# Seven-product matmuls in one pass over all tokens: wider first product, and output halves summed by accumulating transfers

## The chip, the core and the metric

The kernel runs on one core of a Trainium2 chip. The metric is the device time of one execution in microseconds (us). In the profile, PE is TensorE's matmuls, PEld its weight loads, DVE is VectorE, ACT is ScalarE, POOL is GpSimd and SP is SyncE, which here only issues transfers. SBUF is the on-chip memory, PSUM the eight banks into which TensorE writes[...]. "L600" is line 600 of the kernel.

## The reference

A cross attention between the tokens of each batch and a small set of states, and after it an expert block with an activation of its own. All is float32. Shapes: `x` is 8 x 8 x 512 x 64 (batch, head, token, feature of a head), `state` is 8 x 8 x 32 x 64, `w_in` is 512 x 2048, `w_out` is 2048 x 512.

```python
def _attn_ref(x, state):
    scale = 1.0 / np.sqrt(D)
    a = softmax(scale * x @ state.T)              # 512 tokens read 32 states
    xread = a @ state
    a2 = softmax(scale * state @ x.T)             # 32 states read 512 tokens
    sread = a2 @ x
    return concatenate([xread, sread], axis=2)    # 544 rows of each batch

def _moe_ref(x, w_in, w_out):                     # x: 4352 rows of 512
    h = x @ w_in
    sp = np.maximum(h, 0.0) + np.log1p(np.exp(-np.abs(h)))     # softplus
    g = h * erf(sp)
    return g @ w_out
```

(Softmax is written out in the original, with the largest score taken off and 1e-9 added to the sum.)

## The kernel before

Each head has only 32 states, so for the token rows the kernel never forms `xread`. It multiplies the states into the weights, `m = state @ w_in` (256 rows of 2048 for a batch, "mixed"), and then computes `h = a @ m`, the **first product**. The **second product** is `g @ w_out`. Batch 0 runs while the weights are fetched, with plain matmuls. For batches 1 to 7 both products use a scheme for 2 x 2 blocks with **seven products** in place of eight (Strassen in Winograd's form): some sums and differences of the blocks are formed first (S1 to S4 of the left factor, T1 to T4 of the right one), and the seven products are added up to the four quadrants c11, c12, c21, c22 of the result, over partial sums m1, u2 and u3.

A unit of the loop is one batch, one half `h` of its tokens (256) and one half `g` of the expert features (1024): four units for a batch. `hidden7` makes the seven first products of a unit, each of four matmuls of 128 columns into one bank, takes them out of PSUM with ScalarE and VectorE, and applies Softplus. `finish` applies Erf and multiplies. `project7` makes the seven second products, each of four matmuls of 256 columns; they add up over both `g` in the left and right halves of four banks (`acc`), and `store7` takes the banks out once for every two units and writes the output rows. `project7` is a generator: its `yield`s mark the places where the loop puts its steps between the first products of the next unit (`between`), so that TensorE always has something to do. `accompanied` hangs other work (attention of the next batch, mixed weights, sums) at such steps, and `behind` puts instructions after given ones on their engine. The order of the instructions of an engine in this part is set when the program is made, by a scheduler, within what the dependences allow.

```python
    def combine_m(b, g):
        (X11, X12), (X21, X22) = ([m_t[b, 2 * g + j][:, e] for e in range(2)] for j in range(2))
        sx = mix.tile([P, 3, gw], F32, name="sx", bufs=2)
        S1, S2, S4 = (sx[:, k] for k in range(3))
        tt = nc.vector.tensor_tensor
        tt(S1, X21, X22, op=ALU.add)
        tt(S2, S1, X11, op=ALU.subtract)
        tt(X21, X11, X21, op=ALU.subtract)
        tt(S4, X12, S2, op=ALU.subtract)
        X[b, g] = X11, X12, S4, X22, S1, S2, X21
    # ... cut ...
    def hidden7(b, g, h, between, copy=nc.scalar.copy):
        hs = act.tile([P, 4, S], F32, name="hs")
        s = act.tile([P, 4, S], F32, name="s")
        c11, c12, c21, c22 = (hs[:, k] for k in range(4))
        m1, u2, u3 = s[:, 3], c12, c21
        def product(n, bank, first=True):
            x, y = X[b, g][n - 1], Ys[b][n - 1]
            for i in range(GF):
                q = slice(P * i, P * i + P)
                if b < B:
                    ops = [(x[:, q], y[:, h])]
                else:
                    ops = [(x[:, i // 2, k, P * (i % 2):P * (i % 2) + P], y[:, k])
                           for k in range(2)]
                for k, (lhsT, rhs) in enumerate(ops):
                    last = nc.tensor.matmul(out=bank[:, q], lhsT=lhsT, rhs=rhs,
                                            start=(first and i == 0 and k == 0),
                                            stop=(i == GF - 1 and k == len(ops) - 1),
                                            skip_group_check=not first)
            return last
        def softplus(k):
            nc.scalar.activation(out=s[:, k], in_=hs[:, k], func=ACTF.Softplus)
        add = lambda o, x, y: nc.vector.tensor_tensor(o, x, y, op=ALU.add)
        p, q = (ps_h.tile([P, S], F32, name="h") for _ in range(2))
        product(1, p)
        copy(m1, p)
        product(6, q)
        add(u2, m1, q)
        between()
        product(2, p, False)
        copy(c11, p)
        product(7, q, False)
        add(u3, m1, q)
        softplus(0)
        between()
        p, q = (ps_h.tile([P, S], F32, name="h") for _ in range(2))
        product(5, p)
        add(c22, u3, p)
        product(4, q)
        add(c21, u3, q)
        between()
        marks[:] = product(3, p, False), add(c12, u2, p)
        for k in (3, 2, 1):
            softplus(k)
        return s, hs
    # ... cut ...
    def finish(s, hs, parts=(slice(0, GF),)):
        nc.scalar.activation(out=s, in_=s, func=ACTF.Erf)
        for k in parts:
            nc.vector.tensor_tensor(s[:, k], s[:, k], hs[:, k], op=ALU.mult)
    # ... cut ...
    wb = w_out.rearrange("p (g h i) (c e) -> p g h i c e", h=2, i=GF, c=2)
    B11, B12, B21, B22 = (wb[:, :, h, :, c, :] for h in range(2) for c in range(2))
    def project7(gT, hs, g, first, last, acc, order=range(7)):
        blocks = lambda t: [t[:, k].rearrange("p (i t) -> p i t", i=GF) for k in range(4)]
        A11, A21, A12, A22 = blocks(gT)
        S1, S2, S3, S4 = blocks(hs)
        tt = nc.vector.tensor_tensor
        products = ((A12, B21, 0, 0), (A11, B11, 2, 0), (A22, T[4], 1, 0), (S2, T[2], 0, 1),
                    (S3, T[3], 2, 1), (S1, T[1], 1, 1), (S4, B22, 3, 0))
        for n, k in enumerate(order):
            lhs, rhs, bank, c = products[k]
            for i in range(GF):
                if i % 2 == 0 and n:
                    yield
                if i == 2 and n == 1:
                    tt(S1, A21, A22, op=ALU.add)
                    tt(S2, S1, A11, op=ALU.subtract)
                    tt(S3, A11, A21, op=ALU.subtract)
                    tt(S4, A12, S2, op=ALU.subtract)
                nc.tensor.matmul(out=acc[bank][:, E2 * c:E2 * c + E2], lhsT=lhs[:, i, :],
                                 rhs=rhs[:, g, i, :], start=(first and i == 0 and c == 0),
                                 stop=(last and i == GF - 1 and (c == 1 or bank == 3)))
    def store7(acc, put):
        twice = lambda t: t.unsqueeze(1).to_broadcast([P, 2, E2])
        two = lambda t: t.rearrange("p (c e) -> p c e", c=2)
        m1, u3 = (outs.tile([P, E2], F32, name=n) for n in ("m1", "u3"))
        o1, o2 = (outs.tile([P, d_model], F32, name="ot") for _ in range(2))
        c12 = o1[:, E2:]
        add = lambda o, x, y: nc.vector.tensor_tensor(o, x, y, op=ALU.add)
        nc.scalar.copy(m1, acc[2][:, 0:E2])
        add(two(o1), twice(m1), two(acc[0]))
        put(0, o1, slice(0, E2))
        add(u3, c12, acc[2][:, E2:])
        add(two(o2), twice(u3), two(acc[1]))
        put(1, o2)
        add(c12, c12, acc[1][:, E2:])
        add(c12, c12, acc[3][:, 0:E2])
        put(0, o1, slice(E2, d_model))
    def put_x(b, h):
        rows = out[TB * b:TB * b + S].rearrange("(c p) e -> c p e", p=P)
        def go(r, ot, c=slice(0, d_model)):
            nc.sync.dma_start(out=rows[2 * h + r][:, c], in_=ot[:, c])
        return go
    # ... cut ...
    def fast(b, parts, put):
        for h in range(parts):
            box = []
            def project_(gT, k, g, h, box):
                if k == 0:
                    box.extend(tiles(4))
                yield from project7(*gT, g, k == 0, k == 1, box,
                                    (0, 1, 6, 3, 2, 5, 4) if (b, h, k) == (1, 0, 0)
                                    else range(7))
                if k == 1:
                    store7(box, put(h))
            def first(k, g, h, between, *copy):
                gT = hidden7(b, g, h, between, *copy)
                if (b, h, k) == (1, 0, 0):
                    finish(*gT, (slice(2, 4), slice(0, 2)))
                else:
                    finish(*gT)
                return gT
            for k in range(2):
                g = k ^ h ^ begins(b)
                yield lambda *how, k=k, g=g, h=h: first(k, g, h, *how), \
                    lambda gT, k=k, g=g, h=h, box=box: project_(gT, k, g, h, box)
    # ... cut ...
    def accompanied(steps, side):
        for n, _ in enumerate(steps):
            if n in side:
                side[n]()
            yield
    def behind(marks, f, *args):
        with ExitStack() as order:
            for m in marks:
                order.enter_context(tc.issue_after(m.ins))
            return f(*args)
    # ... cut ...
    def pending():
        yield from seconds
        store(acc, lambda r, ot: put_x(0, r // 2)(r % 2, ot))
    for b in range(1, B + 1):
        if b < B:
            groups = fast(b, 2, lambda h, b=b: put_x(b, h))
        else:
            groups = fast(b, 1, lambda h: put_s)
        for g, (first, second) in enumerate(groups):
            side = {}
    # ... cut ...
            steps = accompanied(pending(), side)
            copy = [nc.vector.tensor_copy] if (b, g) == (1, 1) else []
            gT_ = first(lambda: next(steps), *copy)
    # ... cut ...
            done(steps)
    # ... cut ...
            def pending(gT=gT_, second=second):
                return second(gT)
    done(pending())
```

`X[b, g]` and `Ys[b]` are the seven left and right factors of the first product. `s` and `hs` are two buffers each, `ps_h` has two banks, the four `acc` banks one buffer each. `w_in` lies whole in SBUF (64 KB in each partition), `w_out` as well.

Of the kernel before, what the change touches and what calls it, by code (L numbers as in the profile page):

```python
# [16 lines left out]
def kernel(  # L17
# [47 lines left out]

    x_t = {}
# [11 lines left out]
    def in_order(begun):  # L78

        last = {}  # L80
        for i in nc.cur_bb.bb.instructions[begun:]:
# [3 lines left out]
            if i.engine in (nc.tensor.engine, nc.vector.engine, nc.scalar.engine,  # L85
                            nc.sync.engine):
                last[i.engine] = i
# [34 lines left out]
    w_in = const.tile([P, NF // 2, NK, 2 * P], F32, name="w_in")  # L122
# [31 lines left out]
    def weights_in(j):  # L154
        return weight(w_in[:, j],
                      moe_w_in[:, 2 * P * j:2 * P * j + 2 * P].rearrange("(k p) f -> p k f", p=P),
                      (NK, 2 * P))
# [32 lines left out]
    def scored(b, xT):  # L190


        s2 = [ps_at.tile([P, S], F32, name="at") for _ in range(2)]
# [8 lines left out]
    def scores(b, xT):  # L202
        s2 = scored(b, xT)
# [141 lines left out]
    def attention(b, xT=None):  # L345
# [6 lines left out]
        sc, _ = scores(b, xT)  # L352
# [32 lines left out]
        read_tokens(b, a2T, z2, *((ps_h, "h") if 1 < b < B - 1 else ()))  # L385
# [11 lines left out]
    def mixed_pair(b, gs):  # L397

        for g in gs:
            m_t[b, g] = mix.tile([P, 2, gw], F32, name="m")  # L400
        ps = [[pool.tile([P, gw], F32, name=n) for _ in range(2)]
              for pool, n in ((ps_at, "at"), (ps_h, "h"))]
        for k, g in enumerate(gs):
            for i in range(NI):
                for e in range(2):
                    r, q = slice(D * e, D * e + D), slice(Ns * i, Ns * i + Ns)
                    nc.tensor.matmul(out=ps[k][e][q, :], lhsT=st[r, b, q],  # L407
                                     rhs=w_in[r, 2 * g:2 * g + 2, i, :], start=True, stop=True)
        for k in 0, 1:
            nc.scalar.copy(m_t[b, gs[k]][:, 0], ps[k][0])  # L410
            nc.vector.tensor_copy(m_t[b, gs[k]][:, 1], ps[k][1])

    def mixed_part(b, g, j, parts, copy0=nc.scalar.copy, copy1=nc.vector.tensor_copy):
        n = gw // parts
        mg = m_t[b, g][:, :, n * j:n * j + n]
        fs = slice(2 * g + j, 2 * g + j + 2 // parts)
        ps = [ps_at.tile([P, gw], F32, name="at")[:, 0:n] for _ in range(2)]
        for i in range(NI):
            for e in range(2):
                r, q = slice(D * e, D * e + D), slice(Ns * i, Ns * i + Ns)  # L420
                nc.tensor.matmul(out=ps[e][q, :], lhsT=st[r, b, q],  # L421
                                 rhs=w_in[r, fs, i, :], start=True, stop=True)
# [16 lines left out]
    def combine_s(g):  # L439


        (X11, X12), (X21, X22) = ([w_in[:, GF * g + 2 * j:GF * g + 2 * j + 2, 2 * k:2 * k + 2, :]
# [30 lines left out]
    def hidden7(b, g, h, between, copy=nc.scalar.copy):  # L473
# [4 lines left out]
        hs = act.tile([P, 4, S], F32, name="hs")  # L478
        s = act.tile([P, 4, S], F32, name="s")
        c11, c12, c21, c22 = (hs[:, k] for k in range(4))  # L480
        m1, u2, u3 = s[:, 3], c12, c21

        def product(n, bank, first=True):
            x, y = X[b, g][n - 1], Ys[b][n - 1]
            for i in range(GF):
                q = slice(P * i, P * i + P)
                if b < B:
                    ops = [(x[:, q], y[:, h])]
                else:
                    ops = [(x[:, i // 2, k, P * (i % 2):P * (i % 2) + P], y[:, k])  # L490
                           for k in range(2)]
                for k, (lhsT, rhs) in enumerate(ops):
                    last = nc.tensor.matmul(out=bank[:, q], lhsT=lhsT, rhs=rhs,  # L493
                                            start=(first and i == 0 and k == 0),
                                            stop=(i == GF - 1 and k == len(ops) - 1),
                                            skip_group_check=not first)
            return last

        def softplus(k):
            nc.scalar.activation(out=s[:, k], in_=hs[:, k], func=ACTF.Softplus)  # L500
        add = lambda o, x, y: nc.vector.tensor_tensor(o, x, y, op=ALU.add)  # L501
        p, q = (ps_h.tile([P, S], F32, name="h") for _ in range(2))
        product(1, p)
        copy(m1, p)  # L504
        product(6, q)
        add(u2, m1, q)
        between()
        product(2, p, False)
        copy(c11, p)  # L509
        product(7, q, False)  # L510
        add(u3, m1, q)
        softplus(0)
        between()
        p, q = (ps_h.tile([P, S], F32, name="h") for _ in range(2))
# [497 lines left out]
```

## Time and profile before

| | before |
|---|---|
| time, median of 3 runs | 732.3 us (732.28 to 732.37) |
| span of the profiled execution | 730.7 us |
| matmul instructions | 5016 |
| mean granted clock of TensorE | 1.000 |
| transferred | 46.40 MB, of it 8.91 MB written to HBM |
| table loads ahead of Softplus (L500) | 31, 1283 ns each |
| second product at L600 | 1680 instructions of 128x256 |
| first product at L493 | 1792 instructions of 128x128 |

The page gives for each engine its busy time and its share of the span. A busy engine need not be the bound, and an idle one can be: what counts is the chain of work that ended last. The chain is followed back from the last instruction; each piece of it has a start, a length, and the engine and line it belongs to. In a timeline, a row is one or several instructions of a kind in a row; the brackets at its end tell how long the engine was idle before it and what released it. The mean duration of a matmul is from its start to its modelled end and overlaps with the next one, so rates are read from the chain or from a run of many.

### The profile page before, as it was taken

The numbers are of one execution on the slowest core, as the hardware profiler recorded it, in microseconds if no ns is written. First come the engines' busy times: TensorE is split into PE (matmuls) and PEld (weight loads), VectorE is DVE, ScalarE is ACT, GpSimd is POOL, SyncE is SP. The second block draws the span as 40 slices with busy tenths as digits, with TensorE's granted clock in tenths as the row PEclk, the third lists the DMA queues.
The fourth block names the chain that finished last, engine by engine and source line by source line (L and its number), as shares of the span: only waits on it lengthen the run. The fifth ranks groups of instructions, "written<-read, shape, count | busy, mean of one in ns | idle before, by whom it ended". The sixth has DMA issues, their size and how long they took to land.

```text
span 730.7 us, 12128 instructions
## 1 busy us (share of the span) xinstructions
PE 721.6 (99%) x5016; PEld 588.0 (80%) x5016; DVE 524.0 (72%) x766; ACT 395.6 (54%) x498; POOL 0.7 (0%) x6
## 2 busy tenths in 40 slices
PE   8899999999999999999999999999999999999998
PEld 7434435889889888988989888988898899999996
DVE  4988887997798677867587669866686756674423
ACT  4898894665556444754455445544575434443340
POOL 0000000000000000000000000000000000000000
PEclk9999999999999999999999999999999999999999
DMA  7577842330153203310061104220111000000001
GB/s 234 174 216 241 224 94 58 87 59 30 19 99 67 50 1 66 80 30 30 1 144 27 33 1 94 60 44 9 38 50 30 30 1 30 1 30 1 30 1 29
DMA packets 139166, 46.40 MB, mean 64 GB/s; under 512 B 126696, under 2 KB 130536, under 8 KB 139112
## 3 DMA queue, kind: packets, MB, share of 16 engines
q1 hardware_dynamic: 136840, 44.92, 24.6%
q10 hardware_dynamic: 2272, 0.72, 0.5%
q8 instruction: 39, 0.64, 0.4%
q14 instruction: 15, 0.12, 0.1%
HBM read 33.03 MB, written 8.91 MB: 57 GB/s over the span
## 4 chain that ended last, share of the span: by engine, by line
PE 92%; DVE 2%; ACT 1%; issue 0%; ACTq 0%
PE o L600 50%; PE h L493 27%; PE o L550 7%; PE at L407 2%; PE h L407 1%; PE h L714 1%; PE at L197 1%; PE at L421 1%; PE h L277 1%; DVE s L727 0%; PE at L277 0%; DVE hs L721 0%; ACT L724 0%; DVE w_out L148 0%; ACT s L724 0%
## 5 line engine op out<-in xcount | busy, mean ns | idle before, releaser
L600 PE MATMUL o<-w_out,s 128*128 128x256 f32 x480 | 118.0, 380 | 0.0
L600 PE MATMUL o<-raw,hs 128*128 128x256 f32 x480 | 117.3, 382 | 0.0
L500 ACT ACTIVATE s<-hs 128x512 f32<-128x512 f32 x120 | 75.4, 630 | 74.3 <-DVE hs L501 74.0
L600 PE MATMUL o<-w_out,hs 128*128 128x256 f32 x480 | 114.1, 380 | 0.0
L600 PEld LDWEIGHTS o<-raw,hs 128*128 128x128 f32 x480 | 89.9, 190 | 22.6 <-issue 10.9
L501 DVE TENSOR_TENSOR hs<-hs,h 128x512 f32<-128x512 f32 x90 | 61.8, 687 | 62.6 <-PE h L493 62.4
L600 PEld LDWEIGHTS o<-w_out,hs 128*128 128x128 f32 x480 | 90.8, 190 | 16.3 <-issue 4.2
L600 PEld LDWEIGHTS o<-w_out,s 128*128 128x128 f32 x480 | 84.6, 191 | 7.9
L501 DVE TENSOR_TENSOR hs<-s,h 128x512 f32<-128x512 f32 x60 | 41.1, 685 | 67.6 <-PE h L493 67.1
L493 PEld LDWEIGHTS h<-aT,m 128*128 128x128 f32 x672 | 83.8, 192 | 4.3 <-issue 1.4
L493 PE MATMUL h<-aT,m 128*128 128x128 f32 x672 | 84.4, 275 | 0.0
L545 DVE TENSOR_TENSOR s<-s,hs 128x2048 f32<-128x2048 f32 (+1 forms) x31 | 68.8, 2218 | 20.4 <-ACT s L543 20.4
L504 ACT COPY s<-h 128x512 f32<-128x512 f32 x29 | 17.0, 585 | 107.7 <-PE h L493 107.7
L550 PE MATMUL o<-w_out,s 128*128 128x512 f32 x128 | 59.1, 600 | 0.6 <-DVE s L727 0.5
L493 PE MATMUL h<-sy,sx 128*128 128x128 f32 x448 | 59.4, 275 | 0.0
L493 PEld LDWEIGHTS h<-sy,sx 128*128 128x128 f32 x448 | 56.7, 192 | 2.1 <-issue 0.5
L543 ACT ACTIVATE s<-s 128x2048 f32<-128x2048 f32 x30 | 57.4, 1912 | 0.3
L509 ACT COPY hs<-h 128x512 f32<-128x512 f32 x29 | 17.0, 585 | 74.8 <-PE h L493 74.8
L600 PE MATMUL o<-raw,s 128*128 128x256 f32 x240 | 56.8, 379 | 0.0
L550 PEld LDWEIGHTS o<-w_out,s 128*128 128x128 f32 x128 | 23.1, 190 | 31.1 <-issue 25.8
L600 PEld LDWEIGHTS o<-raw,s 128*128 128x128 f32 x240 | 43.5, 190 | 4.7
L500 ACT ACT_TABLE_LOAD x31 | 39.8, 1283 | 0.5
(133 smaller groups left out, 915.4 us busy)
## 6 DMA issues: line engine op xcount, KB each, us to landing
raw<-in_moe_w_in_dram SPq DMA_DIRECT2D x8, 1024.0 KB, 5.7
raw<-in_moe_w_out_dram SPq DMA_DIRECT2D x8, 1024.0 KB, 4.8
xq<-in_x_dram SPq DMA_DIRECT2D x112, 64.0 KB, 2.2
x<-in_x_dram SPq DMA_DIRECT2D x56, 128.0 KB, 2.8
out_dram<-ot SPq DMA_DIRECT2D x18, 256.0 KB, 2.2
sc<-xT SPq DMA_DIRECT2D x112, 32.0 KB, 1.9
out_dram<-ot SPq DMA_DIRECT2D x28, 128.0 KB, 1.9
x<-in_x_dram ACTq DMA_DIRECT2D x2, 256.0 KB, 5.7
```

The lines of the kernel that those rows point to most:

```text
L197: on_pe = nc.tensor.matmul(out=s2[e][q, :], lhsT=st[r, b, q], rhs=xT[r, i, :], start=True, stop=True)
L277: nc.tensor.matmul(out=sr[q, e, :], lhsT=a2T[:, e, c, q], rhs=xt[:, c, 2 * i + e, :], start=(c == 0), stop=(c == NC - 1))
L407: nc.tensor.matmul(out=ps[k][e][q, :], lhsT=st[r, b, q], rhs=w_in[r, 2 * g:2 * g + 2, i, :], start=True, stop=True)
L493: last = nc.tensor.matmul(out=bank[:, q], lhsT=lhsT, rhs=rhs, start=(first and i == 0 and k == 0), stop=(i == GF - 1 and k == len(ops) - 1 ...
L500: nc.scalar.activation(out=s[:, k], in_=hs[:, k], func=ACTF.Softplus)
L501: add = lambda o, x, y: nc.vector.tensor_tensor(o, x, y, op=ALU.add)
L504: copy(m1, p)
L509: copy(c11, p)
L543: nc.scalar.activation(out=s, in_=s, func=ACTF.Erf)
L545: nc.vector.tensor_tensor(s[:, k], s[:, k], hs[:, k], op=ALU.mult)
L550: nc.tensor.matmul(out=acc[r], lhsT=gT[:, i, P * r:P * r + P], rhs=w_out[:, GF * g + i, :], start=(g == 0 and i == 0), stop=(g == NG - 1 a ...
L600: nc.tensor.matmul(out=acc[bank][:, E2 * c:E2 * c + E2], lhsT=lhs[:, i, :], rhs=rhs[:, g, i, :], start=(first and i == 0 and c == 0), stop ...
```

## The change

A unit becomes one batch and one half of the features with **all 512 tokens**: two units for a batch. The first product then streams 256 columns (two runs of 128 from both token halves) over each loaded block of weights, so that half as many matmuls and weight loads of the first product are needed. The unit's `h` fills two of three slots of a new buffer `ring`, one for each half of the tokens. The second product is made for each slot by itself (`project_wide`): one directly (`inner`), the other (`outer`) between the first products of the next unit.

Since both halves of the features of a batch no longer follow each other for the same tokens, the second product doesn't add up over them in PSUM. Each `project_wide` gathers its quadrants in two banks (a and c in one, d and e in the other; two such pairs alternate) and takes them out. For the first half of the features the rows are written as before; for the second they are added to what is there by an accumulating transfer, issued by GpSimd.

The `ring` takes room in SBUF, so only half of `w_in` stays there. Both halves are written out to HBM once they have been converted (`kept_in`), and the half that is wanted next is fetched back. The third `ring` slot holds the other half until then (`away`). TensorE's instructions are now held to the order of the program throughout. Batch 0 keeps its plain matmuls, and more of its second product is left over to the first unit of the loop. The last units, for the rows of the states, keep their form (`hidden_states`, `project7`, `store7`).

The core of the diff:

```diff
+    ring = const.tile([P, 2, 3, GF, GF, P], F32, name="ring")
+    dram = ctx.enter_context(tc.tile_pool(name="dram", bufs=1, space=bass.MemoryType.DRAM))
... (cut) ...
-    def in_order(begun):
+    def in_order(begun, engines=(nc.tensor, nc.vector, nc.scalar, nc.sync)):
... (cut) ...
-    w_in = const.tile([P, NF // 2, NK, 2 * P], F32, name="w_in")
+    w_in = const.tile([P, NF // 4, NK, 2 * P], F32, name="w_in")
+    away = ring[:, :, 2].rearrange("p u k i t -> p u (k i t)").rearrange(
+        "p u (j k f) -> p u j k f", k=NK, f=2 * P)
+    pieces_in = [w_in[:, j] for j in range(NF // 4)] + \
+        [away[:, j // 2, j % 2] for j in range(NF // 4)]
+    of_group = [w_in[:, 2 * g:2 * g + 2] for g in range(2)] + [away[:, u] for u in range(2)]
+    kept_in = dram.tile([2, P, NF // 4, NK * 2 * P], F32, name="kept_in")
     w_out = const.tile([P, NF, d_model], F32, name="w_out")
... (cut) ...
+    def hidden_wide(b, g, low, between, copies):
+        for o in range(2):
+            part = lambda t: [t[:, :, k, 2 * o:2 * o + 2].rearrange("p h i t -> p h (i t)")
+                              for k in range(4)]
+            def product(n, bank, first=True):
+                x, y = X[b, g][n - 1], Ys[b][n - 1]
+                out = bank.rearrange("p (h i t) -> p i h t", h=2, i=2)
+                for i in range(2):
+                    q = P * (2 * o + i)
+                    last = nc.tensor.matmul(out=out[:, i], lhsT=x[:, q:q + P], rhs=y,
+                                            start=(first and i == 0), stop=(i == 1),
+                                            skip_group_check=not first)
+                return last
+            hidden7(part(ring[:, 0, low:low + 2]), part(ring[:, 1, low:low + 2]), product,
+                    lambda t: t.rearrange("p (h u) -> p h u", h=2), between, copies[o])
... (cut) ...
+    def project_wide(n, g, put, more):
+        gT, hs = slot(n)
+        blocks = lambda t: [t[:, k].rearrange("p (i t) -> p i t", i=GF) for k in range(4)]
+        A11, A21, A12, A22 = blocks(gT)
+        S1, S2, S3, S4 = blocks(hs)
+        tt = nc.vector.tensor_tensor
+        add = lambda o, x, y: tt(o, x, y, op=ALU.add)
+        half = n_acc[0] % 2
+        n_acc[0] += 1
+        p, q = (ps_o.tile([P, d_model], F32, name="o%d" % (2 * half + k)) for k in range(2))
+        halves = lambda t: (t[:, 0:E2], t[:, E2:])
+        (a, c), (d, e) = halves(p), halves(q)
+        m1, u3 = (outs.tile([P, E2], F32, name=n) for n in ("m1", "u3"))
+        o1, o2 = (outs.tile([P, d_model], F32, name="ot") for _ in range(2))
+        (c11, c12), (c21, c22) = halves(o1), halves(o2)
+        u2 = c12
+        def product(lhs, rhs, out, start=False, first=True):
+            for i in range(GF):
+                if i == 2:
+                    yield
+                nc.tensor.matmul(out=out, lhsT=lhs[:, i, :], rhs=rhs[:, g, i, :],
+                                 start=(start and i == 0), stop=(i == GF - 1),
+                                 skip_group_check=not (start and first))
+        yield from product(A11, B11, a, True)
+        nc.scalar.copy(m1, a)
+        tt(S1, A21, A22, op=ALU.add)
+        tt(S2, S1, A11, op=ALU.subtract)
+        yield
+        yield from product(A22, T[4], e, True)
+        tt(S3, A11, A21, op=ALU.subtract)
+        tt(S4, A12, S2, op=ALU.subtract)
+        yield
+        yield from product(S2, T[2], c)
+        add(u2, m1, c)
+        yield
+        yield from product(S1, T[1], d)
+        yield
+        yield from product(S3, T[3], c, first=False)
+        add(u3, m1, c)
+        add(c22, u3, d)
+        yield
+        yield from product(A12, B21, a, first=False)
+        nc.scalar.copy(c11, a)
+        add(c21, u3, e)
+        put(1, o2, more=more)
+        yield
+        yield from product(S4, B22, d, first=False)
+        add(c12, u2, d)
+        put(0, o1, more=more)
+    n_acc = [0]
... (cut) ...
-            nc.sync.dma_start(out=rows[2 * h + r][:, c], in_=ot[:, c])
+        def go(r, ot, c=slice(0, d_model), more=False):
+            if more:
+                nc.gpsimd.dma_start(out=rows[2 * h + r][:, c], in_=ot[:, c], accum_op=ALU.add)
+            else:
+                nc.sync.dma_start(out=rows[2 * h + r][:, c], in_=ot[:, c])
         return go
... (cut) ...
+    nc.sync.dma_start(out=kept_in[0], in_=w_in.rearrange("p j k f -> p j (k f)"))
+    for u in range(2):
+        nc.sync.dma_start(out=kept_in[1][:, 2 * u:2 * u + 2],
+                          in_=away[:, u].rearrange("p j k f -> p j (k f)"))
... (cut) ...
-    some(3)
+    some(2)
-    some(4)
+    some(2)
... (cut) ...
+    def bring(o):
+        nc.sync.dma_start(out=w_in.rearrange("p j k f -> p j (k f)"), in_=kept_in[o])
+        for j in range(2):
+            of_group[2 * o + j] = w_in[:, 2 * j:2 * j + 2]
... (cut) ...
+    def halves(gT):
+        s, hs = gT
+        finish_on_act(s)
+        for k in slice(0, 4, 3), slice(1, 3):
+            times(k, gT)
+    turned = []
+    for n, (b, u) in enumerate((b, u) for b in range(1, B) for u in range(2)):
+        o = begins(b) ^ u
+        low = 1 - n % 2
+        inner, outer = 1, 2 * low
+        side, side_a = {}, {}
... (cut) ...
+        steps = accompanied(pending(), side)
+        hidden_wide(b, o, low, lambda: next(steps, None), [nc.scalar.copy] * 2)
+        halves(slot(inner))
+        finish(*slot(outer))
+        done(steps)
+        if n == 0:
+            for k in sorted(side):
+                if k > 6:
+                    side[k]()
+        put = [put_x(b, h) for h in range(2)]
+        done(accompanied(project_wide(inner, o, put[1 - low], u), side_a))
+        if b + 1 < B and ahead:
+            turn = ahead[0]
+        def pending(outer=outer, o=o, put=put[low], u=u):
+            return project_wide(outer, o, put, u)
... (cut) ...
+    in_order(begun, [nc.tensor])
```

The parts cut away adapt names and PSUM pools, hang the attention of the next batches at other steps (`side`, `side_a`), and write `hidden7` so that both uses share it.

## The prediction

> **What bounds the kernel now.** I read the page first, then the chain of work in order of time in the middle of the kernel, then the timeline of each engine over one unit, and last the timeline of the tail. The page's busy times and its chain by engine:
>
> ```profile
> PE 721.6 (99%) x5016; PEld 588.0 (80%) x5016; DVE 524.0 (72%) x766; ACT 395.6 (54%) x498; POOL 0.7 (0%) x6
> ...
> PE 92%; DVE 2%; ACT 1%; issue 0%; ACTq 0%
> ```
>
> TensorE is the bound: it is busy for 99% of the span and makes 92% of the chain. VectorE and ScalarE have room on average, but an average doesn't say that a wait on them is harmless. One unit of the loop in the chain (start, duration, engine, line; L493 is the first product, L600 the second):
>
> ```profile
> 381.34 8.63 PE o L600 x40
> 389.97 1.78 PE h L493 x16
> 391.76 1.73 PE o L600 x8
> 393.49 1.78 PE h L493 x16
> 395.27 0.87 PE o L600 x4
> 396.14 1.78 PE h L493 x16
> 397.92 0.87 PE o L600 x4
> 398.79 0.89 PE h L493 x8
> ```
>
> Each piece begins where the one before ends, so this stage has no hole to win back. It also gives the true rates, which the "mean ns" of the groups (275 and 380) don't, since those are latencies of overlapping instructions. Every float32 matmul appears as two instructions. 40 of them at 256 columns take 8.63 us, 0.2158 us each; 16 at 128 columns take 1.78 us, 0.1113 us each. A unit is 56 of L493 and 56 of L600: 6.23 + 12.08 = 18.31 us, and 28 units make 513 us of the 730.7.
>
> Next, what follows the last L493 product of a unit, on VectorE and ScalarE (from the timelines of the two engines):
>
> ```profile
> 381.38 0.69 DVE L501 TENSOR_TENSOR hs<-hs,h 128x512 f32<-128x512 f32 x1 [1.07 <-PE h L493]
> 382.10 0.63 ACT L500 ACTIVATE s<-hs 128x512 f32<-128x512 f32 x1 [1.13 <-DVE hs L501]
> 382.74 1.28 ACT L543 ACT_TABLE_LOAD   x1
> 384.04 1.91 ACT L543 ACTIVATE s<-s 128x2048 f32<-128x2048 f32 x1
> 386.36 2.28 DVE L545 TENSOR_TENSOR s<-s,hs 128x2048 f32<-128x2048 f32 x1
> ```
>
> In TensorE's timeline that product ends at 381.17. The reader sees a chain of 6 to 7.5 us (add, Softplus, table load, Erf, multiplication) before the next second product has its operand. The 40 instructions (8.63 us) left of the older second product hide it.
>
> Last, the tail, where the second product of the last unit is taken out of its banks (ScalarE, then VectorE and TensorE):
>
> ```profile
> 723.64 0.37 ACT L611 COPY m<-o 128x256 f32<-128x256 f32 x1 [12.70 <-PE o L600]
> ```
> ```profile
> 727.09 0.42 DVE L610 TENSOR_TENSOR ot<-ot,o 128x256 f32<-128x256 f32 x1 [0.71 <-PE o L600]
> ```
> ```profile
> 714.80 3.62 PE L600 MATMUL o<-w_out,s 128*128 128x256 f32 x16
> 718.26 1.89 PE L600 MATMUL o<-raw,s 128*128 128x256 f32 x8
> 719.99 1.89 PE L600 MATMUL o<-raw,hs 128*128 128x256 f32 x8
> 721.71 1.89 PE L600 MATMUL o<-w_out,hs 128*128 128x256 f32 x8
> 723.44 1.89 PE L600 MATMUL o<-raw,hs 128*128 128x256 f32 x8
> ```
>
> The copy at 723.64 reads only the left half of bank 2, A11·B11, which was complete at 718.26 (the second eight of the first row). ScalarE was idle for 12.70 us and still waited until 0.20 us after S3·T3, the product in the right half of the same bank, ended at 723.44. So a wait here belongs to the bank and not to the half. This decides my prediction.
>
> [...] 2 x 0.1113 = 0.2226 against 0.2158, 3%. [...]
>
> **The change, part by part.**
>
> 1. First product at 256 columns. Per half of the features of a batch, 14 products of two 256-column matmuls take the place of two times 7 of four 128-column ones. Per 7 products: 28 x 0.2158 = 6.04 us for 6.23. Saved: 0.19 x 28 = **5.3 us**, all of it on the path, since nothing but TensorE bounds this stage. That is the whole direct gain.
>
> 2. Half of the Softplus/Erf table switches go: about 14 x 2 x 1.28 = 36 us of ScalarE. It is not the bound: **0**.
>
> 3. The second product now gathers its four quadrants in two banks, a and c in one, d and e in the other, and is taken out after every unit (28 times for 14). The order is a, e, c, d, c, a, d. Between S3·T3 into c and A12·B21 into a, both in the same bank, stands the VectorE addition u3 = m1 + c. If waits go by bank, A12·B21 cannot start before that addition has ended, and TensorE is now held to program order, so nothing else comes forward. The wait: 0.20 us from the product's end to VectorE's start (723.44 to 723.64 shows it for ScalarE; VectorE likewise: the last eight matmuls begin at 725.16 and need 1.73, and the addition begins at 727.09), 0.42 us for a 128x256 addition, and some 0.07 us back (an estimate: at 105.11 us TensorE starts about 0.05 us after the first of four multiplications that began at 104.37 and took 2.50 together). 0.69 x 28 = **+19.3 us**. The other places alternate banks, or have 1.7 us of products between read and write.
>
> 4. VectorE may be busy when u3 comes up. It is 72% busy now and gets 5 x 0.42 = 2.1 us per unit where the old store cost 2.6 per two units. Its common operations last 0.4 to 0.7 us, some 1.3 to 2.3. I take 0.2 us on average: 0.2 x 28 = **+5.6 us**.
>
> 5. Between the two halves of the first product, P3 of one is followed at once by P1 and P6 of the next, with two banks for them. One bank has been free since the addition after P4. The other is free 0.20 + 0.69 + 0.07 = 0.96 us after P3, while P1 covers only 0.86: 0.1 x 14 = **+1.4 us**. (If the banks strictly alternate, it would be 0.96 x 14 = 13.)
>
> 6. Start of the loop. After the first pair only one matmul of batch 0 (0.86 us) is left to hide the chain add, Softplus, load, Erf, half multiplication: from 381.17 to 385.95 plus half of 2.28, and 0.1, is 6.0 us. Hole: **+5.2 us**, once. In the other 13 pairs 32 instructions are left, 6.9 us, plus the wait of part 3, 7.6 us: covered.
>
> 7. Four MB of w_in go out to HBM and 2 MB come back per batch. The first must be out before its place is overwritten by the first pair, near 120 us. The queue is free at about 101 us; at the 297 GB/s that the slice of 80 to 90 us shows, this ends at about 115: **0 to 3, taken as +1**. Reloads have a whole half batch (36 us). The accumulating transfers have some 8 us until their buffers are wanted; taken as 0.
>
> Sum: 732.3 - 5.3 + 19.3 + 5.6 + 1.4 + 5.2 + 1 = 759.5.
>
> **Rivals.** (a) No wait by bank in part 3, since the wait at 723.64 could also come from the accumulation group being closed only by the right half's last matmul. Then parts 3 and 4 vanish: 732.3 - 5.3 + 7.6 = about 735, and with the start better hidden than I think 728. I give it one in four. (b) Waits on VectorE and ScalarE become the bound: banks that alternate, a 2.3 us operation in the way of the multiplication, or the accumulating transfers holding the output buffers. For it: VectorE gets more work in exactly the stage where the slack shrinks from 8.6 to 6.9 us. Against it: 28% of its time is free. It would make 770 to 785. (c) The 256-column product is all that matters and the rest is hidden: 727. Against it: parts 3 and 6 leave TensorE nothing to do in program order.
>
> **Range and chances.** Three quarters on about 760 and one quarter on 732 give 753. The range 730 to 771 holds most of rival (a) and the lower edge of (b). Faster than 717.6 would need more than twice the direct gain with no new wait: 0.03. Over 746.9 needs the wait by bank or rival (b): 0.66. The rest is 0.31.
>
> **What would show it.** In the profile of the changed kernel: L493's counterpart at 0.216 us per instruction in the chain (part 1); in each second product a hole of about 0.7 us ahead of A12·B21, released by the VectorE addition u3 (part 3), and chain shares of VectorE well over 2%; a single hole of about 5 us near 138 us (part 6); no hole ahead of the later inner second products; GpSimd's transfers with landing times under 8 us. I am wrong if TensorE runs through from S3·T3 to A12·B21, or if the largest releaser is a DMA or Erf.

## The result and the profile after

| | before | after |
|---|---|---|
| time, median | 732.3 us (732.28 to 732.37) | **901.3 us** (899.54 to 902.41) |
| ratio | | 1.2305, 95% interval 1.2288 to 1.2323 |
| span of the profiled execution | 730.7 us | 900.6 us |
| mean granted clock of TensorE | 1.000 | 0.935 |
| matmul instructions | 5016 | 4232 |

The change costs 169 us where 27 were summed up and 21 predicted. The page of the changed kernel, busy times and chain by engine:

```profile
PE 766.1 (85%) x4232; PEld 583.3 (65%) x4232; DVE 545.4 (61%) x847; ACT 365.5 (41%) x507; POOL 25.0 (3%) x34
...
PE 63%; DVE 23%; SPq 6%; ACT 3%; DMA 2%; issue 2%; ACTq 0%; DVEq 0%
```

TensorE was busy for 99% of the span and is now for 85%; VectorE's part of the chain went from 2% to 23%, although its busy time grew by only 21 us. That points to when VectorE does its work, and not to how much it has; the share of the chain alone proves little (e7 below, 136 us faster, still has 22%). What TensorE waited for, summed over the span (microseconds in total, times, the longest one):

```profile
PE o L642 <- DVE u L627: 55.5, 28, 7.9
PE o L642 <- DVE ot L627: 40.6, 7, 8.0
PE at L284 <- DMA sc<-xT: 21.2, 6, 7.2
PE o L642 <- DVE ring L776: 5.7, 1, 5.7
```

L642 is the second product, L627 the additions that take it out of its banks. The first row has the 28 waits that the prediction expected, one for each A12·B21 (`u` is u3), but 55.5 us for 25. Twelve waits of the first two rows are 3.8 to 8.0 us long; they make 79.6 of these 96 us: five for u3, six for c21 and one for u2. The other 23 are all for u3 and take 0.7 us each on average, the size of part 3.

One of the long ones, in the second half of the features of a batch, from the timeline of all engines (start, duration, engine, line; in brackets the idle time before it and what ended it):

```profile
608.59 1.89 PE L642 MATMUL o<-w_out,ring 128*128 128x256 f32 x8
...
609.72 3.71 ACT L557 ACTIVATE ring<-ring 128x2048 f32<-128x2048 f32 x2
...
611.67 2.35 DVE L776 TENSOR_TENSOR ring<-ring 128x1024 f32<-128x1024 f32 x2
613.94 2.29 DVE L562 TENSOR_TENSOR ring<-ring 128x2048 f32<-128x2048 f32 x1
...
616.75 1.30 DVE L377 STREAM_TRANSPOSE aT<-xT 128x512 f32<-128x512 f32 x2
617.97 0.38 DVE L627 TENSOR_TENSOR u<-m,o 128x256 f32<-128x256 f32 x1
...
618.40 7.85 PE L642 MATMUL o<-w_out,ring 128*128 128x256 f32 x24 [7.93 <-DVE u L627]
```

The product at 608.59 is S3·T3; it is over at about 610.3. u3 takes 0.38 us and could have been made there. It is made at 617.97, because VectorE's queue holds 1.4 us of attention and sums, then the multiplications with Erf (L776 twice, L562: 4.6 us) and 1.9 us more of the next batch's attention (a normalisation and the transposes) ahead of it. TensorE is held to the order of the program and stands still for 7.93 us. VectorE does not wait for Erf meanwhile: in each of the twelve holes it is busy from the hole's first moment to its last.

In the first half of the features, u3 and c22 come in time and another addition is late:

```profile
562.23 0.38 DVE L627 TENSOR_TENSOR ot<-u,o 128x256 f32<-128x256 f32 x1
562.54 2.35 DVE L776 TENSOR_TENSOR ring<-ring 128x1024 f32<-128x1024 f32 x2
...
564.80 2.29 DVE L562 TENSOR_TENSOR ring<-ring 128x2048 f32<-128x2048 f32 x1
...
569.39 0.41 DVE L627 TENSOR_TENSOR ot<-u,o 128x256 f32<-128x256 f32 x1
...
569.86 6.50 PE L642 MATMUL o<-w_out,ring 128*128 128x256 f32 x16 [6.12 <-DVE ot L627]
```

A12·B21 had started at 561.74 after the expected wait, 0.66 us. The next product, S4·B22 into d, shares its bank with e, and c21 = u3 + e still has to read e. c21 is the addition at 569.39. It stands behind the multiplications and 2.5 us of attention, while c22, which uses the same u3, was made at 562.23.

The longest hole, 8.04 us, is at a third place. Here it is u2 = m1 + c that comes late, and S3·T3 is to add to c itself, so that this wait doesn't come from sharing a bank:

```profile
298.11 0.42 DVE L627 TENSOR_TENSOR ot<-m,o 128x256 f32<-128x256 f32 x1
...
298.58 3.78 PE L642 MATMUL o<-w_out,ring 128*128 128x256 f32 x8 [8.04 <-DVE ot L627]
```

The row at 569.86 shows a second loss. Its 16 instructions last until 576.19, 6.33 us, where the rate of before gives 16 x 0.2158 = 3.45. Busy time by stretch, with the granted clock in the column before the last two:

```profile
core 0: us, PE busy (x) PEld busy (x) DVE busy (x) ACT busy (x) POOL busy (x), PEclk, DMA share, GB/s
...
570.00:573.00 3.00, 3.00 (x7) 2.38 (x8) 3.00 (x6) 0.14 (x1) 0.86 (x1) 0.50 0.55 69
...
576.00:579.00 3.00, 3.00 (x16) 2.64 (x14) 0.20 (x1) 0.37 (x1) 0.00 (x0) 1.00 0.74 87
```

After the hole TensorE works at half its clock (0.50, and 0.58 in the 3 us between the two). Eleven of the twelve long holes are followed by one row of 16 or 24 such instructions; over 0.2158 us each, these rows are 1.6 to 3.1 us too long, 25.6 together.

### The profile page after: what moved, and what is told of

It is laid out like the page before. It is cut to its first block, busy times and chain, and to the rows that moved or that the text cites. A ratio compares the mean times of both kernels' runs of the same rounds, so it can differ in the third digit from the quotient of the medians.

```text
span 900.6 us, 10769 instructions
## 1 busy us (share of the span) xinstructions
PE 766.1 (85%) x4232; PEld 583.3 (65%) x4232; DVE 545.4 (61%) x847; ACT 365.5 (41%) x507; POOL 25.0 (3%) x34
## 4 chain that ended last, share of the span: by engine, by line
PE 63%; DVE 23%; SPq 6%; ACT 3%; DMA 2%; issue 2%; ACTq 0%; DVEq 0%
PE o L642 28%; PE h L530 19%; SPq L389 6%; PE o L567 4%; DVE ring L776 3%; DVE ring L562 3%; PE h L545 3%; PE o L617 3%; PE h L414 2%; PE at L414 2%; DMA sc<-xT 1%; PE at L284 1%; PE h L763 1%; DVE xT L224 1%; DVE u L627 1%
## 5 line engine op out<-in xcount | busy, mean ns | idle before, releaser
L642 PE MATMUL o<-w_out,ring 128*128 128x256 f32 x896 | 240.2, 420 | 101.7 <-DVE u L627 55.5
L642 PEld LDWEIGHTS o<-w_out,ring 128*128 128x128 f32 x896 | 186.2, 212 | 146.6 <-DVE u L627 67.0
L497 DVE TENSOR_TENSOR ring<-ring,h 128x512 f32<-128x512 f32 x150 | 103.1, 688 | 166.3 <-PE h L530 139.0
L642 PE MATMUL o<-raw,ring 128*128 128x256 f32 x672 | 162.9, 383 | 0.0
L642 PEld LDWEIGHTS o<-raw,ring 128*128 128x128 f32 x672 | 127.5, 191 | 27.6 <-issue 10.5
L495 ACT ACTIVATE ring<-ring 128x512 f32<-128x512 f32 x120 | 75.6, 630 | 84.7 <-DVE ring L497 84.1
L530 PE MATMUL h<-aT,m 128*128 128x256 f32 x336 | 81.8, 379 | 1.2 <-ACT ring L500 1.2
L567 PE MATMUL o<-w_out,ring 128*128 128x512 f32 x128 | 59.6, 600 | 0.6 <-DVE ring L776 0.5
L530 PE MATMUL h<-sy,sx 128*128 128x256 f32 x224 | 59.0, 386 | 0.0
L557 ACT ACTIVATE ring<-ring 128x2048 f32<-128x2048 f32 x30 | 55.8, 1903 | 0.2
L776 DVE TENSOR_TENSOR ring<-ring 128x1024 f32<-128x1024 f32 (+1 forms) x40 | 42.8, 1111 | 4.2 <-ACT ring L773 4.2
L567 PEld LDWEIGHTS o<-w_out,ring 128*128 128x128 f32 x128 | 23.4, 190 | 30.1 <-issue 25.2
L562 DVE TENSOR_TENSOR ring<-ring 128x2048 f32<-128x2048 f32 x16 | 36.6, 2285 | 3.9 <-ACT ring L557 3.9
L627 DVE TENSOR_TENSOR ot<-ot,o 128x256 f32<-128x256 f32 x28 | 11.7, 417 | 43.9 <-PE o L642 43.9
L627 DVE TENSOR_TENSOR u<-m,o 128x256 f32<-128x256 f32 x28 | 11.5, 412 | 37.0 <-PE o L642 37.0
L500 ACT COPY ring<-h 128x512 f32<-128x512 f32 x30 | 17.3, 578 | 35.8 <-PE h L530 29.4
```

Of the source, the lines that this page charges most:

```text
L495: nc.scalar.activation(out=s[k], in_=hs[k], func=ACTF.Softplus)
L530: last = nc.tensor.matmul(out=out[:, i], lhsT=x[:, q:q + P], rhs=y, start=(first and i == 0), stop=(i == 1), skip_group_check=not first)
L567: nc.tensor.matmul(out=acc[r], lhsT=gT[:, i, P * r:P * r + P], rhs=w_out[:, GF * g + i, :], start=(g == 0 and i == 0), stop=(g == NG - 1 a ...
L627: add = lambda o, x, y: tt(o, x, y, op=ALU.add)
L642: nc.tensor.matmul(out=out, lhsT=lhs[:, i, :], rhs=rhs[:, g, i, :], start=(start and i == 0), stop=(i == GF - 1), skip_group_check=not (st ...
L776: nc.vector.tensor_tensor(gT[0][:, ks], gT[0][:, ks], gT[1][:, ks], op=ALU.mult)
```

## The experiments

All but e11 are edits of the changed kernel or of each other; e11 is e7 with the line that e10 takes out removed. Their order on TensorE is that of the program unless said otherwise. The times of after, e7, e8, e9 and e11 are medians of four runs; the other kernels ran once.

### e1: the additions first on VectorE

c21 is made right after c22, the multiplications for the inner second product are put behind it on VectorE, that for the outer one later still (`hooks` holds the inner ones), and from batch 3 on the part of the next batch's attention that hung at step 8 goes to step 10.

```diff
         add(u3, m1, c)
         add(c22, u3, d)
+        done_e = add(c21, u3, e)
+        while hooks:
+            behind([done_e], hooks.pop(0))
         yield
         yield from product(A12, B21, a, first=False)
         nc.scalar.copy(c11, a)
-        add(c21, u3, e)
```

> Changed kernel, but on VectorE the three additions that free the two banks (u3, c22, c21) stand ahead of the multiplications that wait for Erf; the outer multiplication comes later still. Theory (a wait by bank, made long by VectorE's queue, in which multiplications waiting for Erf stand ahead of the additions): the 13 holes of 3.8 to 8.0 us ahead of A12.B21 or S4.B22 fall to under 1 us, the half-clock stretches after them go, VectorE's other work may open new holes of 2 us ahead of S2.T2; 770 to 800 us. Rival 1 (output buffers held by the accumulating transfers): the holes stay, about 900. Rival 2 (VectorE has simply too much work there): holes move but their sum stays, 880 to 900.

Measured: **859.4 us**, a miss. The waits of TensorE:

```profile
PE at L284 <- DMA sc<-xT: 31.3, 3, 11.3
PE o L642 <- DVE u L627: 22.4, 28, 2.8
PE at L284 <- issue: 21.7, 2, 10.9
```

Eleven of the twelve long holes are gone, so the theory of VectorE's order holds: 96.1 us on `u` and `ot` became 32.0 (22.4, and one wait of 9.6 on `ot`). That one is for u2, which still stands behind the multiplications here. But the attention step that I moved feeds a chain of transfers, and the tokens that read the states (L284) now wait for it: 53.0 us for 21.2. Whether moving that step or moving the multiplications did this isn't separated. One hole was traded for another.

### e2: a bank for each quadrant

```diff
-        p, q = (ps_o.tile([P, d_model], F32, name="o%d" % (2 * half + k)) for k in range(2))
         halves = lambda t: (t[:, 0:E2], t[:, E2:])
-        (a, c), (d, e) = halves(p), halves(q)
+        a, e, c, d = (t[:, 0:E2] for t in tiles(4))
-        yield from product(S2, T[2], c)
+        yield from product(S2, T[2], c, True)
-        yield from product(S1, T[1], d)
+        yield from product(S1, T[1], d, True)
```

> Changed kernel, but a, c, d and e in a bank each, so that no product shares a bank with a quadrant that is being read. VectorE's order as in the changed kernel. Theory: the 0.5 to 1.2 us waits ahead of A12.B21 go, and so do the six long ones on c21 (3.8 to 8.0 us, together about 40 with the half clock after them 55); the six long ones on u3 turn into equally long ones on c22, which is a true dependence: 820 to 845 us. If waits went by quadrant and not by bank: no change, 900.

Measured: **867.2 us**, above the expected range. No wait on u3 is left; the long ones turned into waits on c22, four of them of 7.66 us, as expected. But those on c21 did not go: since the four banks no longer alternate between two projects, the next writer of e's bank, A22·T4 of the next project, meets the late addition (four waits of 3.47 us).

```profile
PE o L639 <- DVE ot L627: 66.1, 13, 8.0
```

So sharing banks is a part of the cause, and not the main one. The waits for the reads grew to 27.2 us. As long as the additions stand behind the multiplications, somebody waits for them.

### e4: plain writes in place of accumulating transfers

This kernel leaves out the sum over the two halves of the features: the second half's rows overwrite those of the first.

```diff
-                nc.gpsimd.dma_start(out=rows[2 * h + r][:, c], in_=ot[:, c], accum_op=ALU.add)
+                nc.sync.dma_start(out=rows[2 * h + r][:, c], in_=ot[:, c])
```

> Changed kernel, but the second half of the features overwrites the rows by plain writes from SyncE in place of the accumulating transfers from GpSimd (it leaves out the sum over the two halves of the features). Theory: the transfers wait for others, not others for them: 895 to 905 us. Rival 1: the long holes go with them, under 800.

Measured: **897.8 us**, 3.4 less than after, whose own runs spread over 2.9. The accumulating transfers are not where the time went.

### e5: useless matmuls in the long holes

24 matmuls of 128x128 whose result nobody reads go ahead of the late product of thirteen outer projects, among them those with the twelve long holes. In the project with the 8.04 us for u2 they stand at another place, and that hole stays.

```diff
+        if idle == 0:
+            busy(24)
         yield from product(S4, B22, d, first=False)
```

(likewise ahead of A12·B21 in the other half)

> Changed kernel, with 24 useless 128x128 matmuls (5.3 us at full clock) put into each of the 12 long holes of TensorE. If the half clock that the trace shows for some 5 us after each long hole comes from TensorE having been idle: the products after the holes run at 0.216 us per instruction again and the kernel gets about 12 x 2.8 = 34 us faster though it does more work, 860 to 875. If the slow stretch has another cause (VectorE or transfers busy then): 898 to 905.

Measured: **894.8 us**; the granted clock rose from 0.935 to 0.973. The total missed, the mechanism holds. The counterpart of the row at 569.86 above:

```profile
564.31 3.72 PE L647 MATMUL o<-w_out,ring 128*128 128x256 f32 x16 [0.77 <-DVE ot L632]
```

It runs at full rate, so the half clock came from the idle time. Such a unit got 2.7 us shorter (24.0 us from 353.69 to 377.72 in after, 21.3 from 352.98 to 374.31 here). In the other half of the features the gain went into a longer wait for the reading tokens' transfers (3.4 us for 2.15), whose end another chain sets.

### e6: e1 with the reads half a batch later

The attention of the next batch is hung half a batch later, so that its transfers have landed some 20 us before TensorE wants them.

```diff
-            reads, scores_of = (True, b + 1) if b < 3 and u == 0 else \
-                (b > 1 and u == 1, b + 2 if b > 1 and u == 1 and b + 2 < B else None)
+            reads, scores_of = (True, b + 1) if u == 0 else (False, None)
```

(and the steps of `turn` at side[3], side[10] and side_a[10] of the half before)

> The kernel with the additions first (two shared banks), and the attention of the next batch one half batch later, so that the product that reads the tokens (waiting for small transfers of the turned weights: 53 us of holes in that kernel) comes some 20 us after those transfers. Theory: these 53 us and the half clock after them go; left are the 28 waits of 0.5 to 1.2 us for u3 (about 22 us), 6 for the start of the loop, and the 9 short ones ahead of S2.T2: 755 to 775 us. Rival (VectorE has too much work): new holes of several us in each half batch, 790 or more.

Measured: **792.5 us**, granted clock 0.989: 17 us over the expected range, and by the time at the rival's edge. But the rival's holes of several us aren't there. Apart from the 5.7 us at the start of the loop the longest wait on the second product is 2.8 us, and the waits for u3 add up to 33.3 us where about 22 were expected:

```profile
PE o L642 <- DVE u L627: 33.3, 28, 2.8
```

The waits for the reads are gone, those for `ot` are down to 0.3 us. Order on VectorE and late reads together were worth 901.3 - 792.5 = 108.8 us.

### e7: e6 with a bank for each quadrant

The banks are given as in e2.

> Additions first, tokens read later, and the four quadrants a, c, d, e in a bank each. Theory: no wait by bank is left, so 732.3 - 5.3 for the wider product + 6 to 9 for the hole at the start of the loop and the clock after it + a few us of rest: 732 to 745 us. If the wait for u3 went by the quadrant, the same as the kernel with two shared banks, 755 to 775.

Measured: **765.4 us** (764.88 to 765.85), ratio 1.045, interval 1.0435 to 1.0466. The separate banks are worth 792.5 - 765.4 = **27.1 us**; parts 3 and 4 of the prediction had 24.9. This is a net figure: the 33.3 us for u3 are gone, and 10.6 have come for banks that no longer alternate. The expectation missed by 20, because many small waits are left, the largest group of them being this (with 5.7 us at the start of the loop and 2.7 on the sums of the left factor):

```profile
PE o L639 <- DVE ot L627: 10.6, 15, 2.0
```

### e8: e7 with the first product at 128 columns

```diff
-                    last = nc.tensor.matmul(out=out[:, i], lhsT=x[:, q:q + P], rhs=y,
-                                            start=(first and i == 0), stop=(i == 1),
-                                            skip_group_check=not first)
+                    for h in range(2):
+                        last = nc.tensor.matmul(out=out[:, i, h], lhsT=x[:, q:q + P],
+                                                rhs=y[:, h], ...)
```

> The kernel with all three corrections, but each 256-column matmul of the first product of batches 1 to 7 made as two of 128 columns, each with its own weight load, as in the kernel before. This measures the direct gain by itself. From the rates in the trace (0.1113 us for 128 columns, 0.2158 for 256): 5.3 us slower than with 256 columns. If the loads of weights were hidden at any width: 0 to 1 us.

Measured: **770.7 us** (769.93 to 770.92), ratio 1.0521, interval 1.0505 to 1.0537, which doesn't touch that of e7. The width is worth **5.3 us**, exactly part 1.

### e9: other work ahead in the first unit

e7 with the pair sums, reads and scores ahead of the inner second product of the first unit, where the hole at the start of the loop is.

> The kernel with all three corrections, and in the first unit the mixing of weights, the reading of tokens and the scores of the next batch (some 4 us of TensorE) put ahead of the inner second product, where TensorE waits for Erf. Theory: the hole of 5.7 us near 142 us shrinks to under 2 us, and the half clock behind it goes: 5 to 8 us faster than without, 727 to 738 us. If the hole is not on the path: no change.

Measured: **765.8 us**, interval of the ratio 1.0441 to 1.0476: the same as e7. The hole only moved:

```profile
146.76 1.10 PE L414 MATMUL at<-w_in,st 64*32 64x512 f32 x7 [6.61 <-DVE st L290]
```

The work put forward needs a VectorE normalisation (L290), and that too stood behind the multiplications waiting for Erf. Whether the start could be filled by something that needs nothing of VectorE was not tried.

### e10: TensorE not held to program order

The changed kernel less its last line; the scheduler may order TensorE as it did before.

```diff
-    in_order(begun, [nc.tensor])
```

> The changed kernel without the last line that holds TensorE to the order of the program; the scheduler may again set TensorE's order as in the kernel before. Theory (the hole comes from VectorE's own order, in which u3 and c21 stand behind multiplications that wait for Erf, and the products of the unit are bound by data and banks anyway): another order of TensorE can only bring other work into the 12 long holes if some is ready; at that place only the inner second product follows, and it needs the very multiplications, so 885 to 905 us. Rival (program order is at fault, because products that are ready are not allowed forward): holes well below 4 us and 800 to 860 us.

Measured: **826.8 us**, granted clock 0.979. The theory as I had put it there is wrong and the rival right: one line is worth 74.5 us. The same place of the same batch as in the first timeline of after:

```profile
568.45 1.99 PE L642 MATMUL o<-w_out,ring 128*128 128x256 f32 x8 [1.45 <-DVE ring L776]
...
573.48 0.38 DVE L627 TENSOR_TENSOR u<-m,o 128x256 f32<-128x256 f32 x1
...
573.91 1.99 PE L642 MATMUL o<-w_out,ring 128*128 128x256 f32 x8 [1.74 <-DVE u L627]
```

u3 (573.48) is still made behind the multiplications. But the inner second product, which needs only the first of them, starts at 568.45 ahead of the outer A12·B21: 1.45 + 1.74 us of holes in place of 7.93. I had said that the inner product needs the very multiplications and so can't help. It needs the first two of them alone (L776, over at 569.5), not all that stands ahead of u3.

In the other half of the features a new wait shows, for the output buffer that an accumulating transfer has not yet released:

```profile
635.19 0.42 DVE L627 TENSOR_TENSOR ot<-m,o 128x256 f32<-128x256 f32 x1 [4.40 <-DMA out_dram<-ot]
...
635.66 2.79 PE L642 MATMUL o<-w_out,ring 128*128 128x256 f32 x8 [3.08 <-DVE ot L627]
```

### e11: e7 without program order on TensorE

> The version of 765.4 us (additions first, reads later, four banks) without the line that holds TensorE to the order of the program. What is left there above 732 are some 35 waits of 0.1 to 1.2 us on VectorE and ScalarE. Theory (these are data waits of a fixed program): 760 to 770. Rival (with other products allowed forward they are filled): 735 to 755.

Measured: **761.6 us** (760.78 to 762.38), ratio 1.0403, interval 1.0385 to 1.042: 3.8 us under e7, as the theory had it. Once VectorE's order is right, the freedom of TensorE is worth little. It isn't that the waits stay: over a whole batch TensorE is now never idle (the stretch from 350.5 to 433.2 us, its length, and then TensorE's busy time),

```profile
350.50:433.20 82.70, 82.70 (x482) 65.70 (x481) 60.71 (x102) 38.29 (x54) 3.45 (x4) 1.00 0.39 83
```

and yet a batch takes 82.8 us for 79.8 before. The small 64x32 matmuls that mix the weights (L414) take part in this: 5.96 us of busy time in this batch, split into groups of 2 to 16; before makes them 16 at a time and has 3.90. No version built here comes below the kernel before.

## Why the prediction was wrong

**Right in kind, and mostly in size.** Part 1: the chain of the changed kernel has the wider first product at 0.216 us per instruction, and e8 puts the gain at 5.3 us.

```profile
163.69 1.73 PE h L530 x8
```

Parts 3 and 4: sharing banks costs 27.1 us in e6 against e7, predicted 24.9; rival (a), no wait by bank, is out. The short waits have the size of part 3, but that the sums agree to 2 us is partly luck, since 27.1 is what is left after new waits came in. Part 5: 0.18 us at the joint of the two halves in the chain (2.77 us at 171.46 us for 12 instructions of the first product, which need 2.59), predicted 0.1. Part 6: one hole at the start, the 5.7 us in the last row of the waits shown above, for 5.2. The later inner products do find their multiplications done, as "covered" said, if only because the outer ones stand still before them. Part 7: there is a wait of 1.16 us near 120 us for 1, but that is luck. The writes of w_in had all landed by 112.5 us; TensorE waits there for a ScalarE copy (L500, 119.72), which runs right behind a copy of batch 0's output. The accumulating transfers land 4.2 us after their issue, and e4 without them is 3.4 us shorter.

**The step that failed** is the last sentence of part 3, "The other places alternate banks, or have 1.7 us of products between read and write", with part 4's 0.2 us on average. The second product has three places of this kind, and I worked out one (u3, with five of the twelve long holes). Another is u2, with one. The third, with six, is c21: it reads e, S4·B22 goes into d in the same bank, and between u3, which c21 needs, and S4·B22 stands one product, A12·B21, 1.73 us. That looked like enough and isn't, since an addition's delay is not the average length of an operation on VectorE. It is all that its queue holds ahead of it at that place, and that is the 4.6 us of multiplications plus up to some 3 us of attention work and sums: at u3 a delay of about 7 us in place of 0.2. The trace of after shows it: u3, ready at about 610.5, ran at 617.97, behind all that the fence above has ahead of it on VectorE.

My rival (b) named this ("a 2.3 us operation in the way of the multiplication") and gave it 770 to 785, because I again counted one operation and not the queue, and because I took 28% of free time on VectorE as evidence against it.

**Terms that were missing.** Three are large. First, the holes themselves: 79.6 us in twelve places. Second, the half clock after them, at least 25.6 us (with all other holes about 38, an estimate: half of the 76 us in which TensorE is busy at half clock by the trace's clock record). My sum had no term for the clock; the trace of after has a stretch at a granted clock of 0.50 at each of the twelve holes, which are 3.8 to 8.0 us long, and the slow rows behind them. Third, the waits of the reading tokens for their transfers (21.2 us; six waits up to 7.2): the attention of the next batch was hung at steps that suited the old pace, and I didn't follow that chain at all.

**The 169 us, by what the experiments took away.** Order on VectorE and late reads, 108.8 (after to e6; they aren't separated, as e1 shows that moving one moves the other); shared banks, 27.1 (e6 to e7); what e7 still has over before, 33.1, which includes the direct gain of 5.3. These remaining 38.4 us are only partly named. By the pages of before and e7, TensorE is idle for 30.6 us in place of 9.1, which makes 21.5, the 5.7 at the start among them. The other 17 are busy time: 733.0 us for 721.6, though the wider product takes 5.3 off. In a batch in the middle (a period of 83.1 us against 79.8 less the gain of 0.8) only 1.8 of the 4.1 us too much are idle time. What makes the busy time longer there was not tried. e10 shows that the first 108.8 are not due to VectorE's order alone: a hole needs a late addition *and* a TensorE that may not pass it. Taking away either fills most of it.

## What to carry to other kernels

When a change puts reads of accumulators between the products of an engine that runs in order, don't ask how busy the reading engine is on average: list, from its timeline at that place, what its queue holds ahead of each read, with the waits of those operations, and set this against the products that stand between read and next write. Forcing one engine's order while another's is left to a scheduler is a change of its own, and here the dearest (74.5 us for one line). A gain of 5.3 us in rate is soon spent: each of the long holes here cost 1.6 to 3.1 us of clock on top of itself.

## What the hardware showed unexpectedly

Two holes of the same length at the same place of two batches in e6, in TensorE's timeline:

```profile
467.07 3.72 PE L642 MATMUL o<-w_out,ring 128*128 128x256 f32 x16 [1.95 <-DVE u L627]
...
553.30 5.41 PE L642 MATMUL o<-w_out,ring 128*128 128x256 f32 x16 [1.95 <-DVE u L627]
```

The first is followed at full rate, the second by 1.8 us lost to the half clock. Busy time by stretch in the second hole (its first row here) and behind it, with the granted clock in the column before the last two:

```profile
core 0: us, PE busy (x) PEld busy (x) DVE busy (x) ACT busy (x) POOL busy (x), PEclk, DMA share, GB/s
...
551.00:553.00 2.00, 0.35 (x2) 0.00 (x0) 2.00 (x4) 0.00 (x0) 0.00 (x0) 1.00 0.00 0
553.30:555.00 1.70, 1.70 (x7) 1.48 (x8) 1.70 (x6) 0.00 (x0) 0.47 (x1) 0.84 0.15 26
555.00:557.00 2.00, 2.00 (x6) 1.60 (x5) 1.71 (x3) 0.37 (x1) 0.39 (x1) 0.50 0.75 71
557.00:559.00 2.00, 2.00 (x9) 1.65 (x8) 0.26 (x1) 0.00 (x0) 0.00 (x0) 0.78 0.97 160
```

The like over the timelines of after and of all experiments but e8, for holes of 0.3 us or more ahead of products of 256 columns (counted as slow when the row that follows takes over 0.5 us more than its rate):

| hole | number | followed by a slow stretch |
|---|---|---|
| under 1.5 us | 197 | 3 |
| 1.5 to 3 us | 26 | 9 |
| over 3 us | 51 | 51, by 0.9 to 3.1 us |

The loss doesn't grow with the hole in the trace of after: 1.8 us after the one of 3.8, 1.6 to 3.0 after those of 6 to 8.

So in these runs the length of a hole alone does not decide. Of the holes of 1.5 to 3 us, 9 of 26 were followed by a slow stretch, and of these two of 1.95 us one. What made the difference between them was not shown.
